# Attention and a maxout feed-forward on one core: the first four chunks' scores by pairs of heads, head 0's transposes first, and a new written order

## The chip, the core and the metric

The kernel runs on one core of a Trainium2 chip. The metric is the device time of one execution in microseconds (us). Three runs of the kernel before took 449.90, 450.04 and 452.39 us, median 450.04. The engines are named as in the profile: PE (TensorE matmuls; PEld its weight loads), DVE (VectorE), ACT (ScalarE), POOL (GpSimd) and SP (SyncE, which issues most DMAs; its queue is SPq).

## The reference

Eight batches, eight heads, 576 positions, 64 values per head, all float32.

```python
scores = scale * np.matmul(q, k.transpose(0, 1, 3, 2))
thresh = np.max(scores, axis=-1, keepdims=True) - tau          # tau = 0.02
scores = np.where(scores >= thresh, scores, -1000000000.0)
scores = scores - np.max(scores, axis=-1, keepdims=True)
attn = np.exp(scores)
attn = attn / (np.sum(attn, axis=-1, keepdims=True) + 1e-09)
attn_out = np.matmul(attn, v)
x = attn_out.transpose(0, 2, 1, 3).reshape(4608, 512)
h = np.maximum(np.maximum(x @ w1, x @ w2), x @ w3)              # 512 -> 768
out = h @ w_out                                                 # 768 -> 512
```

## The kernel before

**Tiles.** The work of attention comes in 16 quads, a quad being four heads of one batch. In a quad, r (0 or 1) is a pair of heads and i (0 or 1) the head in the pair, so the head is 2r + i. The 576 queries of a head are nine blocks of 64. A quad has nine chunks of 128 query rows: chunks 0 to 3 are four double blocks of i = 0, chunk 4 is the ninth block of both i, chunks 5 to 8 are i = 1. Each chunk has two tiles, one for each pair r: 128 queries by 576 keys. That makes 288 tiles.

**Steps of a quad.** `load` fetches q and k (the main eight blocks, and the ninth blocks in a transfer of their own) and v (`vm`, and the rests `vr`). `transposed` turns q or k of one pair on PE into a PSUM bank; `evacuated` copies it to SBUF, q by ACT with the scale (`qt`), k by DVE (`kt`). `swapped` has POOL copy `qt` to `qs` with the two halves of the partitions exchanged. `scores` then makes a tile from `kt` with `qt` and `qs`.

**Softmax of a tile.** A tile goes one of two ways, as the string `MASKED` says. Either way DVE takes the row maximum from PSUM ("m", `maximum`) and ACT makes a first pass ("e", `exponents`). For a tile with a 1 (masked) the second pass is on DVE ("k", a `scalar_tensor_tensor`); for a tile with a 0 it is on ACT ("n", an `activation` with an accumulator). DVE takes the reciprocals of a chunk's two sums ("r"), POOL normalizes both tiles into `P` ("p"), SP sends a DMA transpose of `P` to `ptq` ("t"). A tile's buffer `z` is used again four chunks later (`ZBUFS`), once POOL has read it.

**After attention.** `product` ("O") multiplies `ptq` with v; its copies ("x" on ACT, "w" on DVE) make `xt`. `ffn` has 18 hidden pieces for each part of a batch ("F", second half "B"; PE `ph`), whose copy "h" is ACT's and whose maxima "v" are DVE's, and output pieces (`po`, copies "u" on ACT, stores "o"). "g" loads a weight piece, "z" casts it on POOL, "y" casts v on POOL, "l" issues one load of a later quad. The last batch is split in two parts (`SPLIT`).

**Order.** `ORDER` is a string of these letters. The kernel goes through it and issues each step; S, T, O and F carry the number of the PSUM bank they use (four banks, each of 128 x 1024 float32). The helper `_Ordered` chains the instructions of each engine, so every engine runs its own in the order of the string, and an instruction that waits holds up all behind it on its engine. S takes the next tile, T the next transposes ("a" is then the copy of q, "c" of k, "q" one of the swaps). Every recorded instruction has line 90 in the profile, so groups are told apart by tile names.

**The start.** Ahead of `ORDER`, 14 warming transposes (`WARM`) run on PE, the first quad is loaded (`load(0, first=True)`: q on SP, k on ACT's queue), and all of its transposes are written out: q and k of pair 0, then 5 more warming ones (`FILL`), then q and k of pair 1, each with its copies and swaps. One swap copy of the first quad is DVE's, and one k copy is ACT's. The string starts with a weight load and the second quad's loads; the second quad's first transposes (T0) stand behind four score tiles.

Of the kernel before, what the change touches and what calls it, by code (L numbers as in the profile page):

```python
# [24 lines left out]
101000100110000110011100001010010001100010001000101000010000100000100010  # L25
000011110101100001001001001001000001011100101011000110001010010000010011
001010011101100000101100100001001010000110011111000001000100000110000101
001001001101100000110001000100101000001100010011100101110110000001111111
# [4 lines left out]
FILL = 5  # L33
# [6 lines left out]
glllllS0lylS1mylyeS2zmlkS3lelmnlT0mS1aS2rmeqS0meqmeS3pnkT1pT0nrcaptemS0yeS1mgS2eympeS3mqtnT1S0mqnS2knrceprmS  # L40
1epkepeS3mnyS0rkptemnS2pmnlzmS3erremtpT0empS1eklpaS2kgnS0ptnmeprrmlS1epS3mleS2pmlS0eplmetpmeS1knS3tkernkS2pt
nmnprmtepmS1eqS0melpmT2ntrmT3pnrcpatekS3pekS2eqnrS1mtnqmS0pemepS3tmeqS2kepT1lnrcnprtmS0nT1pmS3epmgS2atpmeO1k
yermeO0knptrerT3wpnT2cS1aptmnS3pS2xmptS1emzS0emeS3zgmeS2lrmpnS0lmO1eplmeplknO3qlnrwleplkS1xqgS2ertmF3npF0meT
1pBrteBkyhS2cpnS3mpS1nvF2npmF0eqBmeqBrrvepS3tkhT2pS1nmS0lapmetS2pmeS3mzeF0mF1ezgBrnF2vpgnBktByeF0rvhpS3ntS2p
mF1npmBeBqrveT3zncT0F2taqvS3nBpmnS0tprhS1rmpeS3mtpS2emeyS0mteF1zmeF3kBelqBnvgF2pngT0vBnqlrS1cphS3lrmnS0plmO2
eplmeptS1ewpS3nmF0znmS2lBezkgO3etymyS1vegkF0ntF2nrrmpBxBpveS3phS0mtnF1prmeBprS2evptS3nmF0pnS1mplBermS3ztnS2v
nzS1meS0tmpeF3mperkS2petBmepmS0tkuF1ukelkT3elBkntrarmpS2uS3pmulS0eymtO1empnrO2kpewS3xpS1elmpF2lmF0eyqBrlkeT3
ytBhcF1pnT2vT3qlaBclnS0qvlS2nqtF3mnyF1meS0pBemBthrrF2kpeS3vnBpmF0nS1pveBrprS3mhtS2pmeS0pmeS1tpmF2emF3peBtkeT
0BvaF1onvqT2T0tBcqaS3nkqS0lhrmS2nlpmF1elpF3meBlkBelF0vntS2rvnBpS1mhplS3melF0mS2teBrmepS1rkpO3emnqO2tnrvpnwyS
0xlprS3emoF2pmoT1eyBpctS3evyF0nS1mtnS2pmBeympF1hkS3eyF2rekT0ptBamBnpS0veF3qtvS1urmnpS2mF3epketT0nkT1Bnrmparr  # L50
cpS2uS1pumtS0empS3emqoS1eF2mqlemqleS3kplnS0mBlepmlekT1teO3kunktO0urcpnrrwlS2nplS1xmpS3lmpS0eompS1eF2mtpeF3me
BkBetS0khF1nrmF2pnBvpBerrvS3phS0mtnpS1mF2peS3mtpeBmeF1yvF0etByknBvnS2tS3rhmpS1melpS0meF3lmF2elBkeBlvT1ntF0nv
T3BacS2ohS1rrmlpnF3lmF0peoBkpeBovnT2oS1qavS3tnprO2rmpmleqS0wtnT3pS1mepO2mteqkeqF0nS1cxBympnS3rS2hytmS1emF0pe
F3mpeBrkBpetF2vnF1pBnvS0thkS3nmF2BmeBveF0rrvpT1uS3kapS0nmS2F1pmtepmeS3rktepS0mnS2pmlBelrmeplS3kupS0lurmS2elp
F1mnoqmeS0qreS2lmpS3elmBpelmptekO0nketO2ukurrnwpT3T1xpcS0aF2ymyT3tpS1ceBqmS3thqF0meF2pknBtBnvF1nS3rtrvpeBmS0
phS2lmepS1lmyS3etF0meyF2mpeBkBetF1knF3vnBBrvhpS0nvT1pF2nmF3takBeS0rvplBmS1phlrS2remplF3mpleF0klBpeS1lvnS2lpm
nBtrO3mepvnptS2nwS1emF0mF3eBrkepS2hBrmS1nptvS0npT2meO3qmeycqlT0xT1yS2lacF3ntmyT0yeF1kqBatrBrevqF0hkS2pnoS3mF
1pmBteBpveS2qntS0vpnF3mprS1mlueS3pmoS0nqmtF2epmekT1oBerocpetrkS3npS1nmS0lpumS3uopmS1eT2mF0aokeorS3remplS2emt
pS1emBpeklqtkO3uqunO0rtmpewpT2xtS3cpeS0mnF2tF1meBknF3lkBhlBevF2nS0vnBmS1hrrS3pmeF0pmS2eBpmteF1pveF3kBlnS0vnl
S2rrBnmlpS1hrlmpF0eF3mtpeBkpBevtS2nF1pvnT0pBtmaS3hS0metF1rmepT2BrcepS3nvptT0S2nmyS1amS3lepmS0leO2mlelmeO1rkp  # L60
ewnT3pF0xcF2nykBnS1vnBrmS3phF0rrmepS2BynmqF1levF3qlBekpF0onvS2tBqmBhqrS1lepvT2S3lampF0lmS2peoBkpetF1vnS3prmu
S0ntqmS1eF2pmetpmeS3rkepS1tBmnpmelrS0keptS3muS1uymS0temT2yeF3pcntknT2BkelramtpS1nS2pmuS0leqrmO1tuqrkepO3nwep
mS1xpS2metF3pmS0eqBmeF1yhrkT2pBtecF3nS0vpnlS2rmpS1nlmBpnF0lveS2tmF3eBmeBkleF1klhF2lnrBvplS0nrrvptBnS3mphS1my
teS2mF3epmF0eBpeBtvpT1nrS2yvnlS3maF0omnqS1kBepF3temS2hpBrrmeS0ptveS1pmS3nptS2meO0pmeymnqlO3weokeoF1xkT0tT2S3
rcapBnmlF2pnS0vqtBerrmpS1hF3mqeT2BpncF0evptF2nkBpT1nvBlaS3ylS0hmoF1yqmT2eoBqrcnF0tpS3ervT2pBmaF1ytkqS2uvnS3q
mS1epF0mepmeS2kteT3BrnrcponmpS1uryS3umtS2emF0pepomeS1opnS2mtpeO3myektnO1wnkS2xrS3repmS1mpBekpteS2muS3purmF1e
pF0tmeBpkS3ntBhS2rnmpO1empO3xvS2xtnkS1eF3rmpF0emByepBveF1tkS2hS3mBmF0eF2rvepBBpvS1htkO3nmO0xkS2xeS3rmF0pF1me
pBeBtvS2F3vF0mF1kBeBkhF2nrvBpnBrvpS3hS0ptmS1pmeS2mtnF0mF3eBrnpBvnF1pS2vntS0rmpBmF3phoS2eS0omeF1tmBeBkO2vO0rv
pF3kpF1uketeF3kekBwrrkpBukxpuF2F0hptF1vF2pvF0hF1tvF2rvpF0hF1vpF2vF0thF1uvF2uvF0hoF3vF1vF2hoF0voO3oO1wovF2xF3
uoF0F1hF2vF0vF1hF2vF0vF1hF2vF0vF1hF2vF0vF1hF2vF0vF1hF2vBvF0uuooBF1uuuooo  # L70
# [31 lines left out]
def kernel(  # L102
# [22 lines left out]
    nc = tc.nc  # L125
# [56 lines left out]
    def load(g, first=False):  # L182
        b, qd = quads[g]
        L = Ls[g] = dict(b=b, qd=qd, first=first)
# [7 lines left out]
        q2 = nc.scalar if first else sync  # L192
        srcs = (("q", q, sync), ("k", k, q2))
        if first:
            for n, src, e in srcs:
                e.dma_start(out=L[n][:, 0:8], in_=rows_of(src)[:, 0, 0:8])
        for n, src, e in srcs:
            e.dma_start(out=L[n][:, 8:10], in_=rows_of(src)[:, :, 8])
            yield
        for n, src, e in srcs:  # L200
            if first:
                e.dma_start(out=L[n][:, 10:18], in_=rows_of(src)[:, 1, 0:8])
            else:
                e.dma_start(out=L[n].rearrange("p (r c) d -> p r c d", r=2)[:, :, 0:8], in_=rows_of(src)[:, :, 0:8])
            yield
# [37 lines left out]
    def swapped(L, r):  # L243

        cols = slice(320 * r, 320 * r + 64 * (5 - r))
        for x in (1, 0) if L["first"] else (0, 1):
            e = vector if L["first"] and (r, x) == (0, 0) else pool
            e.tensor_copy(out=L["qs"][64 * x:64 * x + 64, :, cols],
                             in_=L["qt"][64 - 64 * x:128 - 64 * x, :, cols])
            yield  # L250
# [7 lines left out]
    def transposed(L, n, r):  # L258
# [3 lines left out]
        nj = 5 - r  # L262

        def first(where):
            st["ps"] = ps = bank("tp", where)
            main = ps.rearrange("p (i z) -> p i z", i=2)[:, :, 0:256].rearrange("p i (jj u x) -> p i jj x u", jj=2, x=2)
            for j in range(nj):
                for i in (1, 0):
                    rows = slice(64 * i, 64 * i + 64)
                    tensor.transpose(main[:, i, j // 2, j % 2] if j < 4 else ps[:, 512 * i + 256:512 * i + 320],  # L270
                                     couple(L, n, r, j, rows), identf[rows, rows])
# [435 lines left out]
```

## Time and profile before

| | |
|---|---|
| median of three runs | 450.04 us (449.90 to 452.39) |
| profiled execution, its own time | 449.93 us |
| its span, first to last instruction | 448.1 us |
| DMA | 87.44 MB, mean 195 GB/s |
| q and k loads of 512 KB | 4.7 and 5.1 us from issue to landing (medians) |
| DMA transposes of P | 144, 4.2 us to landing (median) |
| mean granted PE clock | 0.988 |

The span is what the profile sees; the 1.83 us to the execution's own time lie around it. Group rows name an operation by "out<-in". Times in timelines are from the span's start: start, length, engine, operation, and in brackets how long the engine had been idle and what released it.

### The profile page before, as it was taken

To read this page: it belongs to the slowest core of one execution; us is meant where nothing else is said; L and a number is where in the kernel's file an instruction comes from. 1 tells how busy PE (TensorE), PEld (TensorE's weight loads), DVE (VectorE), ACT (ScalarE), POOL (GpSimd) and SP (SyncE) were. 2 spreads that over 40 slices of the span, in tenths; PEclk is the share of its full clock that TensorE was granted. 3 is DMA by queue.
4 is the path that set the end of the run, shared out by engine and by line. 5 is a ranking of instruction groups with operands and counts; after the bars stand their busy time and mean duration, and the time that the engine had idled before them with its cause. 6 is when DMAs were issued, how large, how long until landed. Compare 5 with 4: busy or idle time off the path is not lost.

```text
span 448.1 us, 14065 instructions
## 1 busy us (share of the span) xinstructions
PE 427.0 (95%) x5195; PEld 317.6 (71%) x5195; DVE 399.4 (89%) x1101; ACT 392.4 (88%) x793; POOL 314.2 (70%) x417
## 2 busy tenths in 40 slices
PE   7766889999999999999999999999999999999995
PEld 6524647767688768878687867868687787787762
DVE  3799999899999999999999999999999999999641
ACT  3899999999899999999999999999999999866422
POOL 3798889989785985587776785659777787534400
PEclk9898899999999999999999999999999999999999
DMA  8989999999999999999999997999998999546722
GB/s 235 266 195 188 234 238 190 249 244 220 250 192 193 187 236 209 207 215 179 227 175 205 228 217 176 217 230 205 197 195 203 204 156 194 108 78 132 130 95 107
DMA packets 212773, 87.44 MB, mean 195 GB/s; under 512 B 185824, under 2 KB 199648, under 8 KB 212704
## 3 DMA queue, kind: packets, MB, share of 16 engines
q1 hardware_dynamic: 212000, 85.69, 94.6%
q8 instruction: 41, 0.67, 0.6%
q10 hardware_dynamic: 704, 0.85, 0.6%
q14 instruction: 28, 0.23, 0.2%
HBM read 34.60 MB, written 9.44 MB: 98 GB/s over the span
## 4 chain that ended last, share of the span: by engine, by line
PE 77%; DVE 7%; ACT 5%; POOL 3%; DMA 3%; issue 2%; SPq 1%; DVEq 0%; POOLq 0%; ACTq 0%
PE ph L90 30%; PE sc L90 28%; PE po L90 10%; PE o L90 7%; ACT z L90 5%; DVE z L90 4%; PE tp L90 3%; DVE unused L90 2%; POOL P L90 2%; DMA qm<-in_q_dram 1%; DMA km<-in_k_dram 1%; SPq L90 1%; DVE hm L90 1%; DMA out_dram<-ob 1%; DVE kt L90 0%
## 5 line engine op out<-in xcount | busy, mean ns | idle before, releaser
L90 POOL TENSOR_SCALAR P<-z,rs 128x576 bf16<-128x576 f32 x288 | 228.8, 809 | 89.2 <-DVE rs L90 45.2
L90 PE MATMUL sc<-kt,qs 64*128 64x256 f32 (+2 forms) x640 | 180.5, 423 | 7.7 <-DVE z L90 2.0
L90 PE MATMUL sc<-kt,qt 64*128 64x320 f32 (+2 forms) x640 | 181.1, 433 | 4.0 <-DVE kt L90 1.2
L90 PE MATMUL ph<-xt,w 64*128 64x288 bf16 (+2 forms) x2160 | 165.5, 283 | 0.4 <-DVE hT L90 0.2
L90 PEld LDWEIGHTS <-w 64*128 64x128 bf16 (+1 forms) x2160 | 127.3, 94 | 29.8 <-issue 7.2
L90 ACT ACTIVATE z<-sc,nm 128x576 f32<-128x576 f32 x179 | 128.9, 740 | 10.8 <-DVE unused L90 9.5
L90 DVE TENSOR_SCALAR_CACHE_REDUCE unused<-sc 128x576 bf16<-128x576 f32 x179 | 130.5, 751 | 8.2 <-PE sc L90 7.3
L90 ACT ACTIVATE z<-z 128x576 f32<-128x576 f32 x179 | 120.8, 680 | 0.1
L90 PEld LDWEIGHTS sc<-kt,qs 64*128 64x128 f32 (+1 forms) x640 | 92.3, 179 | 30.9 <-ACT z L90 7.8
L90 PEld LDWEIGHTS sc<-kt,qt 64*128 64x128 f32 (+1 forms) x640 | 92.2, 178 | 20.0 <-ACT z L90 5.4
L90 DVE SCALAR_TENSOR_TENSOR z<-z 128x576 f32<-128x576 f32 x109 | 89.1, 832 | 0.2
L90 DVE TENSOR_SCALAR_CACHE_REDUCE z<-sc 128x576 f32<-128x576 f32 x109 | 80.5, 752 | 7.9 <-PE sc L90 4.6
L90 ACT ACTIVATE z<-z,nm 128x576 f32<-128x576 f32 x109 | 81.5, 772 | 2.6 <-DVE z L90 2.0
L90 POOL COPY qs<-qt 64x512 f32<-64x512 f32 (+1 forms) x63 | 45.0, 714 | 15.0 <-ACT qt L90 11.9
L90 PE MATMUL po<-wo,hT 64*128 64x512 bf16 (+1 forms) x480 | 54.0, 356 | 0.1
L90 DVE TENSOR_TENSOR hm<-ph,hm 128x576 bf16<-128x576 f32 (+2 forms) x54 | 37.1, 687 | 11.7 <-PE ph L90 11.3
L90 ACT ACTIVATE hm<-ph 128x576 bf16<-128x576 f32 (+2 forms) x54 | 32.1, 595 | 15.2 <-PE ph L90 13.7
L90 PEld LDWEIGHTS <-hT 64*128 64x128 bf16 (+1 forms) x480 | 29.3, 97 | 17.0 <-issue 3.1
L90 DVE TENSOR_TENSOR hT<-ph,hm 128x576 bf16<-128x576 f32 (+2 forms) x54 | 37.2, 688 | 3.8 <-PE ph L90 0.9
L90 PE MATMUL o<-ptq,vb 128*64 128x512 bf16 (+2 forms) x544 | 38.9, 282 | 0.2
L90 ACT ACTIVATION_READ_ACCUMULATOR z<-z 128x1 f32 x179 | 35.4, 198 | 0.0
L90 PEld LDWEIGHTS <-vb 128*64 128x64 bf16 x544 | 23.5, 111 | 14.4 <-issue 4.4
(33 smaller groups left out, 278.2 us busy)
## 6 DMA issues: line engine op xcount, KB each, us to landing
vm<-in_v_dram SPq DMA_DIRECT2D x32, 256.0 KB, 4.2
out_dram<-ob SPq DMA_DIRECT2D x31, 256.0 KB, 2.8
qm<-in_q_dram SPq DMA_DIRECT2D x15, 512.0 KB, 4.7
km<-in_k_dram SPq DMA_DIRECT2D x15, 512.0 KB, 5.1
stage<-in_moe_w_dram SPq DMA_DIRECT2D x9, 512.0 KB, 4.5
ptq<-P SPq DMA_TRANSPOSE x144, 4.2
stage<-in_moe_w_out_dram SPq DMA_DIRECT2D x3, 512.0 KB, 4.9
qm<-in_q_dram SPq DMA_DIRECT2D x16, 64.0 KB, 2.9
```

The lines of the kernel that those rows point to most:

```text
L90: ins = fn(*a, **kw)
```

## The change

- The order of tiles: the first four chunks have all their r = 0 tiles first (tiles 0 to 3), then their r = 1 tiles; from chunk 4 on the two tiles of a chunk follow each other as before.
- Ahead of the string only head 0 (r = 0, i = 0) of the first quad is transposed: q without its ninth block (4 transposes) and k (5). Then come 6 warming transposes (`FILL`, before 5), and the two swaps of these columns. The rest of the first quad comes by T in the string: head 2, then heads 1 and 3, six steps of 4 or 5 transposes. So the first quad has eight smaller copies out of PSUM where it had four.
- All k copies are DVE's and all swaps POOL's, also in the first quad.
- The first loads of the first quad: each queue sends pair 0's main blocks first; then SP sends q's pair 1 ahead of q's ninth blocks, and ACT's queue k's ninth blocks ahead of k's pair 1.
- `MASKED` (107 ones in place of 109) and `ORDER` are new throughout.

```diff
-FILL = 5
+FILL = 6
...
-glllllS0lylS1mylyeS2zmlkS3lelmnlT0mS1aS2rmeqS0meqmeS3pnkT1pT0nrcaptemS0yeS1mgS2eympeS3mqtnT1S0mqnS2knrceprmS
+glS2llS3mlyS0lemlT1emlT2akT3elqcT1qlaT0qlcS2aqgT3nzS1lcnT0mS3qgamqeS0qmeS1ymT2ynqkT0eS3ncarmT2peS0mpermpetS1
...
+            for x in range(3):
+                for n, src, e in (("q", q, sync), ("k", k, nc.scalar)):
+                    if x == 0:
+                        e.dma_start(out=L[n][:, 0:8], in_=rows_of(src)[:, 0, 0:8])
+                    elif (x == 1) == (n == "k"):
+                        e.dma_start(out=L[n][:, 8:10], in_=rows_of(src)[:, :, 8])
+                    else:
+                        e.dma_start(out=L[n][:, 10:18], in_=rows_of(src)[:, 1, 0:8])
...
-        elif L["first"] and r == 1:
-            scalar.activation(out=dst(L["kt"]), in_=src, func=AF.Copy)
...
+    def blocks(n, r, ii):
+
+        if n == "q" and ii == (0,):
+            return ((0, 1, 2, 3), (4, 0, 1, 2, 3))[r], 256 * r
+        return ((0, 1, 2, 3, 4), (0, 1, 2, 3))[r], 320 * r
+
+    def swapped(L, r, ii=(0, 1)):
+
+        js, off = blocks("q", r, ii)
+        cols = slice(off, off + 64 * len(js))
+        for x in (0, 1) if len(ii) == 2 else (1, 0):
+            pool.tensor_copy(out=L["qs"][64 * x:64 * x + 64, ii[0]:ii[-1] + 1, cols],
+                             in_=L["qt"][64 - 64 * x:128 - 64 * x, ii[0]:ii[-1] + 1, cols])
             yield
...
+    tiles = [(n, r) for r in range(2) for n in range(4)] + [(n, r) for n in range(4, len(steps)) for r in range(2)]
+    place = {x: n for n, x in enumerate(tiles)}
...
-    for x, (r, n) in enumerate(((0, "q"), (0, "k"), (1, "q"), (1, "k"))):
-        p = transposed(Ls[0], n, r)
+    for x, n in enumerate("qk"):
+        p = transposed(Ls[0], n, 0, (0,))
         p.first(x)
         p.done[0]()
...
+    for _ in range(FILL):
+        tensor.transpose(warm[:, 0:128], identf, identf)
+    for _ in swapped(Ls[0], 0, (0,)):
+        pass
...
-                T=((g, n, r) for g in range(1, NQ) for r in range(2) for n in "qk"),
+                T=iter([(0, n, 1, (0,)) for n in "qk"] + [(g, n, r, (0, 1) if g else (1,)) for g in range(NQ) for r in range(2) for n in "qk"]),
```

More of the change, by code (lines that the diff above doesn't have):

```diff
@@ L45 @@
[L45 to L54, printed above, removed]
@@ L256, in targets, with transposed @@
                 L["qs"] = qk.tile([128, 2, S], F32, name="qs")
-    def transposed(L, n, r):
+    def transposed(L, n, r, ii=(0, 1)):
         st = {}
-        nj = 5 - r
+        js, off = blocks(n, r, ii)
+        lead = 64 if js[0] == 4 else 0
         def first(where):
             st["ps"] = ps = bank("tp", where)
-            main = ps.rearrange("p (i z) -> p i z", i=2)[:, :, 0:256].rearrange("p i (jj u x) -> p i jj x u", jj=2, x=2)
-            for j in range(nj):
-                for i in (1, 0):
+            main = ps.rearrange("p (i z) -> p i z", i=2)[:, :, lead:lead + 256] \
+                .rearrange("p i (jj u x) -> p i jj x u", jj=2, x=2)
+            for j in js:
+                for i in ii[::-1]:
                     rows = slice(64 * i, 64 * i + 64)
-                    tensor.transpose(main[:, i, j // 2, j % 2] if j < 4 else ps[:, 512 * i + 256:512 * i + 320],
+                    ninth = 512 * i + (0 if lead else 256)
+                    tensor.transpose(main[:, i, j // 2, j % 2] if j < 4 else ps[:, ninth:ninth + 64],
                                      couple(L, n, r, j, rows), identf[rows, rows])
@@ L553, with pieces_of_scores @@
         pass
[L554 to L555 removed]
+    for x, n in enumerate("qk"):
+        p = transposed(Ls[0], n, 0, (0,))
         p.first(x)
         p.done[0]()
[L558 to L570 removed]
+    for _ in range(FILL):
+        tensor.transpose(warm[:, 0:128], identf, identf)
+    for _ in swapped(Ls[0], 0, (0,)):
+        pass
+    def pieces_of_scores():
+        for n, r in tiles:
+            if n == len(made):
+                g, idx = steps[n]
+                made.append(dict(g=g, idx=idx, n=n))
+            yield made[n], r
     def pieces():
```

117 lines of the change are left out of this document (52 added, 65 removed).

## The prediction, as it was put on record

> **What bounds the kernel now.** I read the page first, then the table of windows, the timeline of the first 22 us, the chain of waits and the order of both kernels' instructions on each engine. The page:
>
> ```profile
> span 448.1 us, 14065 instructions
> ...
> PE 427.0 (95%) x5195; PEld 317.6 (71%) x5195; DVE 399.4 (89%) x1101; ACT 392.4 (88%) x793; POOL 314.2 (70%) x417
> ...
> PE   7766889999999999999999999999999999999995
> ...
> PEclk9898899999999999999999999999999999999999
> ```
>
> PE is busy 427.0 of 448.1 us. Its 21 idle us lie at the two ends. Windows place them:
>
> ```profile
> 20.00:57.00 37.00, 27.69 (x237) 17.11 (x232) 35.96 (x109) 36.60 (x77) 32.79 (x42) 0.91 1.00 202
> 57.00:70.00 13.00, 11.63 (x135) 7.13 (x136) 12.46 (x36) 12.62 (x27) 11.55 (x15) 1.00 1.04 232
> 70.00:100.00 30.00, 29.64 (x372) 21.25 (x366) 28.40 (x74) 29.24 (x63) 27.93 (x36) 1.00 1.15 226
> 100.00:443.70 343.70, 343.18 (x4334) 260.47 (x4332) 311.76 (x855) 302.46 (x611) 232.04 (x309) 1.00 0.94 187
> ```
>
> Columns: stretch, length, busy PE, PEld, DVE, ACT, POOL, granted clock, DMA share, GB/s. From 100 to 443.7 us PE idles 0.52 us: no order can gain more there. From 20 to 57 us PE idles 9.31 us, ACT only 0.40 and DVE 1.04: the softmax of the first 50 score tiles bounds, because the feed-forward matmuls (first at 67.9 us) are not yet to be had. Whatever brings ACT and DVE through these tiles sooner brings the end nearer, one for one. The last 4.4 us are the output.
>
> Before that comes the start:
>
> ```profile
> 9.40 0.78 ACT L90 ACTIVATE z<-z,nm 128x576 f32<-128x576 f32 x1 [0.55 <-DVE z L90]
> 10.74 0.74 ACT L90 ACTIVATE z<-sc,nm 128x576 f32<-128x576 f32 x1 [0.56 <-DVE unused L90]
> 11.51 0.68 ACT L90 ACTIVATE z<-z 128x576 f32<-128x576 f32 x1
> 12.10 0.19 ACT L90 ACTIVATION_READ_ACCUMULATOR z<-z 128x1 f32 x1
> 13.99 0.70 ACT L90 ACTIVATE qt<-tp 128x640 f32<-128x640 f32 x1 [1.70 <-PE tp L90]
> ```
>
> ```profile
> 11.00:13.40 2.40, 0.00 (x0) 0.00 (x1) 1.94 (x7) 1.26 (x3) 1.98 (x3) 1.00 0.94 333
> 13.40:17.00 3.60, 3.57 (x26) 3.30 (x28) 1.79 (x5) 3.01 (x5) 2.03 (x3) 0.61 1.11 332
> ```
>
> By 13.99 us ACT has done two first passes (e, 0.78 and 0.74) and one second pass (n, 0.68; its accumulator read overlaps, so instructions in a row are 0.67 to 0.69 apart). Then it, DVE and PE stand behind the second quad's first transposes, whose q lands at 13.29:
>
> ```profile
> 0.74 4.12 DMA km<-in_k_dram
> ...
> 7.90 5.39 DMA qm<-in_q_dram
> 13.29 0.14 issue
> 13.43 0.53 PE tp L90 x10
> ```
>
> **The change, part by part.**
>
> *First scores.* Before, 10 q and 10 k transposes run from 4.64 (0.064 apart), 5 warming ones from 5.95 to 7.21 (0.25 each), then 16 more transposes, and the first score matmul at 7.81, its maximum on DVE at 8.60. After: 4 q and 5 k transposes, 6 warming ones, scores. The k transfer lands at 4.86, so transposes end at about 4.9 + 5 x 0.064 = 5.2 (5.95 if the ninth block's transfer comes as late as the old transposes could hide). Copies: DVE kt took 0.82 at 640 columns and 0.67 at 512, so 0.45 at 320; ACT qt 0.70 and 0.60, so 0.39 at 256; POOL qs 0.71 and 0.61, so 0.41. kt and the first qs half are ready near 6.1, hidden under the warming ones, which end at 5.2 + 6 x 0.25 = 6.7. Scores start at 6.7 (bounds 6.1 and 7.5), the first maximum at 7.5: 1.1 us sooner.
>
> *ACT up to 13.99.* The transfer that ends at 13.29 doesn't move: SP issues the same kinds of transfer in the same places up to it (three q, two v, two v rests, weights, two rests, q). Only q's two last pieces of the first quad swap; they are wanted at about 8 us, and the old first quad's were in use by 7.2. The new ACT order ahead of that wait is e, e, three q copies of the remaining heads, an e among them, and two n. From 8.2: 5 x 0.68 + (0.44 + 0.44 + 0.39) = 4.7, done at 12.9, before 13.99. So three e and two n are done where there were two and one: ACT leads by 2 x 0.68 = 1.36 us (bounds: 0 if k is 1.4 late, 1.36). The kt copy taken off ACT (0.59) and the split q copies (1.66 for 1.30) fall into idle time: 0.
>
> *DVE.* Four kt copies (0.45, 0.37, 0.45, 0.37) replace one of 0.82 and a qs copy of 0.52: +0.3, in time in which DVE idled (1.16, 0.57 and 1.88 us). Five maxima are done by the wait, not four: lead 0.68.
>
> *POOL.* Eight qs copies, 4 x 0.41 + 4 x 0.46 = 3.5 us, for 0.71 + 1.28 = 2.0: +1.5. POOL idled 1.7 us just before the second quad's copy at 14.82, and the first normalization (16.40) stood behind that copy before as after. 0; without that gap up to 1.5.
>
> *Masks.* 107 of 288 tiles are masked, not 109. It is the early part that counts: 15 and 14 in the first two groups of 48 tiles, before 17 and 16. Each tile unmasked puts an n on ACT (0.68 in a row) and takes a second pass of about 0.75 from DVE. At tile 48 ACT has 1.36 more and DVE 1.5 less to do; at tile 96 twice that.
>
> *Net at the first feed-forward matmul.* ACT: 1.36 - 1.36 = 0. DVE: 0.68 + 1.5 = 2.2 sooner. The two wait for each other (in the chain ACT z carries most of 34 to 45 us, DVE z of 49 to 60), so the bounds are 0 and 2.2 and I take the middle: -1.1. From 57 to 100 us ACT gets 1.36 more and has 0.38 + 0.76 = 1.14 idle: +0.2.
>
> *The rest of the order.* It is rewritten throughout, but tile counts hardly move: first product at tile 40 in both, first feed-forward piece at 50, the 30th at 98, the 100th at 215. From 100 us on, bounds -0.5 and, for new waits, the largest of the rows of this stage, about +2; I take 0. At the end two products and two pieces go ahead of the last scores, so the last softmax has about 17.4 - 1.4 - 1.7 = 14.3 us of PE work to hide under. It needs three maxima and four second passes (4.9), some 1.6 of maxout, two normalizations (1.5) and a DMA transpose (4.2): 12.2. Covered by 2.1; 0.
>
> Sum -0.9. The profiled execution took 449.93 us (span 448.1 and 1.8 around it), 0.11 under the median of 450.04. 449.93 - 0.9 = 449.0.
>
> *A rule against it.* PE idles 2.57 us before 13.43 and is granted only 0.61 of its clock until 17, and score matmuls of 0.38 and 0.43 take 0.63 and 0.74; pairs come 0.53 apart instead of 0.27. The new order has many short waits from 8 to 13 us in place of one long one, so the clock could fall sooner. The Trainium skill (TensorE: Matmul & The Clock Gate, What's actually happening) has the clock halve after an idle window of about 3.4 us; the trace agrees in kind, but here a wait of 2.57 us was enough. By that rule the clock would hold, since no wait so long is left, and the sum stay at 449.0; by the row it can still fall, at the price of the clock rival below.
>
> **Rivals.**
>
> *All of the lead arrives.* If DVE was the true limit up to 57 us and ACT's idle time takes in its extra passes, the gain is the 2.2 plus the part of the start that is not in it (1.1 - 0.68): 2.6, 447.3 us. For: DVE ends most waits from 49 to 60. Against: ACT's 36.60 of 37.
>
> *ACT becomes the limit (slower).* Place: tiles 1 to 96. If nothing of DVE's relief counts, ACT ends them 4 x 0.68 - 1.36 = 1.36 later: 451.3. It decides from the point where ACT's idle time up to 100 us (1.5 us now) is used up. For: ACT at 99% from 20 to 57 us. Against: idle 0.76 at 70 to 100.
>
> *A late k load.* The third quad's main k transfer stood ahead of the first DMA transpose on SP (issued at 14.84); now it stands behind three, each of which waits for POOL's P, so it goes at about 25 us and lands at 30 to 31 (5.1 to 6.1 by its own rows). Its transposes come after tile 22, near 31 to 32; behind them PE's scores and so DVE and ACT queue. From a landing at 33 on each us costs one. 452 with 2 us.
>
> *The clock.* Eight tiles at 0.53 a pair for 0.27, two pairs each, 4.2 us if PE bounds then: up to 453.2. Against: DVE needs about 1.4 a tile, so PE has room for slow scores.
>
> *The change does not do what it says:* if the ninth block of k lands so late that scores still start near 7.8, only masks and order are left, and ACT's 1.36 is not repaid: 451.3, as above.
>
> **How the numbers follow.** Forecast 449.0 (its own range 448.0 to 450.4): 0.47. Whole lead, 447.3: 0.22. ACT as the limit, or no earlier scores, 451.3: 0.14. Late load, 452: 0.08. Clock, 453.2: 0.04. Something in the new order that I don't see, of either sign: 0.05. 446.0 to 452.5 holds all but some 0.15. A measurement of this kernel tells about 1%, 4.5 us, from no change: faster than 445.5 takes more than any case gives, 0.05; slower than 454.5 the clock's worst or an unseen stall, 0.06; within, 0.89.
>
> **What would show it.** First score matmul at 6.7 and first maximum at 7.5; three e and two n on ACT ahead of the second quad's q copy, still at about 14; ACT over 99% busy from 20 to 57; first feed-forward matmul 0 to 2 us sooner than 67.9; PE idle after 100 us still near 0.5; no PE wait for km near 31. I am wrong if the first feed-forward matmul moves by more than 3 us, if PE idles over 2 us from 100 us to its last matmul, or if the final product waits for a DMA transpose.

## The result, and the profile after

The kernel after takes 454.49 us (median of 12 runs, 451.18 to 455.98). Twelve runs of the kernel before on the same chip have a median of 450.69 us. The ratio is 1.0073, with a 95% interval of 1.0047 to 1.0099: slower by 3.3 us going by the ratio (0.0073 x 450.7) and 3.8 by the medians, where 1 us less was forecast. The profiled execution took 453.53 us (before 449.93), so the two profiles differ by 3.6 us and can be held side by side.

The page of the after:

```profile
span 451.7 us, 14092 instructions
...
PE 429.6 (95%) x5196; PEld 311.1 (69%) x5196; DVE 400.7 (89%) x1099; ACT 394.3 (87%) x798; POOL 314.2 (70%) x422
...
PE   8776889999999999999999999999999999999995
...
PEclk9987999999999999999999999999999999999998
```

The first slice is fuller than before (8 for 7), as it was meant to be, and so is the third (7 for 6); the second and the fourth are as they were. What has changed on the path that sets the end is in the shares of the chain, first the before's, then the after's:

```profile
PE ph L90 30%; PE sc L90 28%; PE po L90 10%; PE o L90 7%; ACT z L90 5%; DVE z L90 4%; PE tp L90 3%; DVE unused L90 2%; POOL P L90 2%; DMA qm<-in_q_dram 1%; DMA km<-in_k_dram 1%; SPq L90 1%; DVE hm L90 1%; DMA out_dram<-ob 1%; DVE kt L90 0%
```

```profile
PE ph L90 29%; PE sc L90 28%; PE po L90 10%; ACT z L90 8%; PE o L90 8%; PE tp L90 3%; DVE z L90 2%; DVE unused L90 1%; DMA qm<-in_q_dram 1%; DMA km<-in_k_dram 1%; POOL P L90 1%; SPq L90 1%; DVE hm L90 1%; DMA out_dram<-ob 1%; DVE kt L90 0%
```

ACT's passes over z hold 8% of the chain instead of 5%, DVE's z, its unused and POOL's P half of what they held. The stretches that were shown of before (busy PE, PEld, DVE, ACT, POOL, granted clock, DMA share, GB/s):

```profile
20.00:57.00 37.00, 27.89 (x218) 16.63 (x218) 34.93 (x103) 35.62 (x75) 34.67 (x43) 0.86 1.01 208
57.00:70.00 13.00, 10.83 (x122) 6.32 (x119) 11.98 (x28) 11.89 (x26) 10.68 (x14) 1.00 0.80 190
70.00:100.00 30.00, 29.20 (x375) 21.79 (x373) 27.61 (x74) 29.85 (x65) 27.15 (x37) 1.00 1.06 232
100.00:447.20 347.20, 345.93 (x4355) 254.59 (x4351) 313.90 (x861) 304.29 (x613) 231.86 (x309) 1.00 0.92 184
```

From 20 to 57 us ACT and DVE are each busy 1 us less than before (35.62 for 36.60, 34.93 for 35.96): they wait more. POOL has become full too (34.67 for 32.79). After 70 us PE idles 0.80 + 1.27 = 2.07 us, before 0.36 + 0.52 = 0.88.

The difference at PE's end (447.28 for 443.71 us, +3.57) adds up so: the first feed-forward copy on ACT starts at 72.06 for 69.96, +2.10; PE idles 1.19 more after 70 us; 0.28 is left for everything else.

**The start** did what was forecast in this execution (in half of those profiled it did not, see the last section). ACT's timeline:

```profile
8.39 0.78 ACT L90 ACTIVATE z<-z,nm 128x576 f32<-128x576 f32 x1 [2.58 <-DVE z L90]
9.07 0.73 ACT L90 ACTIVATE z<-sc,nm 128x576 f32<-128x576 f32 x1
...
10.02 0.74 ACT L90 ACTIVATE z<-sc,nm 128x576 f32<-128x576 f32 x1
...
11.60 0.68 ACT L90 ACTIVATE z<-z 128x576 f32<-128x576 f32 x1
...
12.27 0.67 ACT L90 ACTIVATE z<-z 128x576 f32<-128x576 f32 x1
...
13.87 0.70 ACT L90 ACTIVATE qt<-tp 128x640 f32<-128x640 f32 x1 [0.84 <-PE tp L90]
```

Three e and two n ahead of the second quad's q copy, which waits for a transfer that hasn't moved (chain of the after):

```profile
0.74 4.10 DMA km<-in_k_dram
7.87 5.30 DMA qm<-in_q_dram
```

Windows of the same stretch: PE is busy 3.82 us of 5.20 where it did nothing for 2.4, and its clock here stays whole until 17 us (0.61 before).

```profile
8.00:13.20 5.20, 3.82 (x40) 2.72 (x36) 4.36 (x14) 4.42 (x10) 3.73 (x6) 1.00 1.00 313
13.20:17.00 3.80, 3.19 (x40) 2.43 (x40) 2.89 (x7) 3.13 (x6) 2.98 (x7) 1.00 1.02 299
```

**Where the lead goes.** Starts of the same instruction, after less before, in the profiled executions (us):

| | DVE m | ACT e | POOL P |
|---|---|---|---|
| 1st | -1.01 | -1.01 | +2.00 |
| 16th | -2.73 | -1.15 | -0.62 |
| 24th | -1.25 | +0.88 | -1.93 |
| 36th | +0.12 | +1.69 | -1.27 |
| 44th (m), 50th (e) | +1.48 | +2.10 | |

DVE is 2.7 us ahead at its 16th maximum, and ACT 1.15 ahead at its 16th first pass (28.2 us). By 37.8 us ACT is behind. Two places can be seen. In the first, PE, ACT and the clock (PE's timeline of the after, then ACT's, then a window):

```profile
29.02 0.55 PE L90 MATMUL sc<-kt,qs 64*128 64x320 f32 x1 [2.09 <-ACT z L90]
...
31.74 0.75 PE L90 MATMUL tp<-identf,qm 64*128 64x64 f32 x9
```

```profile
32.64 0.70 ACT L90 ACTIVATE qt<-tp 128x640 f32<-128x640 f32 x1 [0.73 <-PE tp L90]
```

```profile
29.40:32.80 3.40, 3.40 (x31) 2.48 (x28) 3.15 (x10) 2.43 (x7) 3.20 (x5) 0.50 0.98 234
```

PE waits 2.09 us for a bank that ACT's first pass gives back, is granted half its clock from 29.4 to 32.8, and its third-quad transposes come late for ACT, which stands 0.73 us. The second place is DVE's, beside POOL (DVE's timeline, then POOL's):

```profile
57.57 3.15 DVE L90 SCALAR_TENSOR_TENSOR z<-z 128x576 f32<-128x576 f32 x1
60.65 0.75 DVE L90 TENSOR_SCALAR_CACHE_REDUCE unused<-sc 128x576 bf16<-128x576 f32 x1
```

```profile
55.35 2.80 POOL L90 TENSOR_SCALAR P<-z,rs 128x576 bf16<-128x576 f32 x3
58.09 1.03 POOL L90 CAST w<-stage 128x1024 bf16<-128x1024 f32 x1
59.08 1.04 POOL L90 CAST vb<-vm 128x1024 bf16<-128x1024 f32 x1
```

One second pass k takes 3.15 us for some 0.75. It starts inside POOL's last P, and ends 0.6 us behind the second of two casts that follow that P without a gap. The k before it started at 55.31, just ahead of POOL's P at 55.35, and took 0.77; there POOL's three P's take 2.80 where they need 0.75 each. The Trainium skill (SBUF — State Buffer, SBUF: two separate sides) says that DVE, with two inputs in SBUF, and a POOL instruction that reads SBUF share one port pair: whichever starts first locks it for its whole instruction, and the other waits outright. The trace agrees where two start together: the k that started first kept its length (0.77) and POOL's P's beside it took 2.80 for 2.25; the k that started inside a P took 3.15. That this pass lost the pair to the two casts as well, which started after it, is an inference from where it ends.

**What ACT's time to its 50th first pass consists of** (sums over the trace, us):

| | e | n | qt, kt copies | idle | 50th e at |
|---|---|---|---|---|---|
| before | 32.69 | 19.34 (29) | 5.25 | 9.69 | 69.33 |
| after | 32.54 | 21.35 (32) | 4.88 | 10.30 | 71.42 |

(The table load and two xt copies, 2.36 us, are the same in both.) Three more n are 2.01 us. Idle time is up by 0.61 although the start took off 1.01, so 1.6 of waits are new. ACT's timeline shows where they are: from 20 us on it idles 2.47 us (before 0.77). Of these 0.73 is the gap at 32.64 above, 0.33 and 0.24 are waits for DVE at 47.34 and 29.84, and 1.11 comes behind the long second pass of DVE:

```profile
61.50 1.42 ACT L90 ACTIVATE z<-sc,nm 128x576 f32<-128x576 f32 x2 [1.11 <-DVE unused L90]
```

DVE, to its 50th maximum: 14 k for 17, yet 15.56 us for 14.64 (1.11 each for 0.86), and k copies 5.75 for 4.17. The relief that was forecast for DVE is not there at all.

### The profile page after: what moved, and what is told of

It reads as the page before. It is cut to its first block, busy times and chain, and to the rows that moved or that the text cites. A ratio compares the mean times of both kernels' runs of the same rounds, so it can differ in the third digit from the quotient of the medians.

```text
span 451.7 us, 14092 instructions
## 1 busy us (share of the span) xinstructions
PE 429.6 (95%) x5196; PEld 311.1 (69%) x5196; DVE 400.7 (89%) x1099; ACT 394.3 (87%) x798; POOL 314.2 (70%) x422
## 4 chain that ended last, share of the span: by engine, by line
PE 78%; ACT 9%; DVE 5%; issue 3%; DMA 3%; POOL 1%; SPq 1%; DVEq 0%; POOLq 0%; ACTq 0%
PE ph L90 29%; PE sc L90 28%; PE po L90 10%; ACT z L90 8%; PE o L90 8%; PE tp L90 3%; DVE z L90 2%; DVE unused L90 1%; DMA qm<-in_q_dram 1%; DMA km<-in_k_dram 1%; POOL P L90 1%; SPq L90 1%; DVE hm L90 1%; DMA out_dram<-ob 1%; DVE kt L90 0%
## 5 line engine op out<-in xcount | busy, mean ns | idle before, releaser
L90 PE MATMUL sc<-kt,qs 64*128 64x320 f32 (+2 forms) x640 | 182.1, 423 | 6.3 <-ACT z L90 5.0
L90 PE MATMUL sc<-kt,qt 64*128 64x256 f32 (+2 forms) x640 | 182.0, 433 | 5.5 <-ACT z L90 4.4
L90 PEld LDWEIGHTS <-w 64*128 64x128 bf16 (+1 forms) x2160 | 126.0, 94 | 32.1 <-issue 6.8
L90 ACT ACTIVATE z<-z 128x576 f32<-128x576 f32 x181 | 122.1, 680 | 0.2
L90 DVE SCALAR_TENSOR_TENSOR z<-z 128x576 f32<-128x576 f32 x107 | 91.0, 864 | 0.0
L90 ACT ACTIVATE z<-z,nm 128x576 f32<-128x576 f32 x107 | 79.8, 773 | 9.4 <-DVE z L90 9.1
L90 DVE TENSOR_SCALAR_CACHE_REDUCE z<-sc 128x576 f32<-128x576 f32 x107 | 78.9, 752 | 10.0 <-PE sc L90 7.2
L90 POOL COPY qs<-qt 64x640 f32<-64x640 f32 (+3 forms) x68 | 46.9, 690 | 11.6 <-ACT qt L90 8.2
L90 PE MATMUL po<-wo,hT 64*128 64x512 bf16 (+1 forms) x480 | 52.9, 356 | 0.1
L90 ACT ACTIVATE hm<-ph 128x576 bf16<-128x576 f32 (+2 forms) x54 | 32.0, 593 | 17.2 <-PE ph L90 16.7
L90 PEld LDWEIGHTS <-hT 64*128 64x128 bf16 (+1 forms) x480 | 26.3, 97 | 20.1 <-issue 3.7
```

The lines of the kernel that those rows point to most:

```text
L90: ins = fn(*a, **kw)
```

## Experiments

All are compared with the before, run beside them; the after stands at 1.0073 [1.0047, 1.0099]. Tiles are counted from 0.

### Parts of the change, alone

Four tiles (9, 20, 31, 44) of the before unmasked, so that four second passes go from DVE to ACT, in their old places:

```diff
-101000100110000110011100001010010001100010001000101000010000100000100010
+101000100010000110010100001010000001100010000000101000010000100000100010
```

> The kernel before with four tiles of the first 48 (tiles 9, 20, 31 and 44) taken from the masked way to the other one, each at its old place in the order: four second passes move from DVE to ACT. Theory A (ACT alone sets the pace of the first 100 us, so each second pass on it costs its 0.68 us): 2.7 us slower than before, and the 50th first pass on ACT 2 to 2.7 us later than the 69.3 us of before. Rival B (the loss lies in stalls of the new order, not in the masks): within 0.7 us of before.

Measured: 453.69 us, ratio 1.0064 [1.0041, 1.0087]. To the 50th e ACT's n take 21.97 us (before 19.34), and that e starts at 71.81, +2.5. DVE's k fall to 13 and 10.0 us; DVE idles instead (17.2 us for 11.1). More n on ACT reach the end in full, and DVE's relief is worth nothing: theory A's number.

The opposite in the before, tiles 12, 23, 33 and 43 masked:

> The opposite of the four-more experiment: in the kernel before, tiles 12, 23, 33 and 43 get the masked way, each second pass at its old place, so four of them move from ACT to DVE. Theory A (ACT alone sets the pace of the first 100 us): up to 2.7 us faster than before, 448 us. Rival D (the written order is balanced so finely that any departure from it, either way, costs about 3 us, and the count on ACT has no part in it): slower than before by 1 to 3 us.

Measured: 451.85 us, ratio 1.0039 [1.0014, 1.0065]. ACT's n fall to 16.81 us, but its idle time rises from 9.69 to 14.00. Theory A alone is false: ACT now waits for DVE instead (5.3 us for its z, unused and rs from 8 to 75 us, before 1.7). Rival D's number (1 to 3 us slower) is met too; the next run decides on it. Two each way (20 and 31 unmasked, 23 and 33 masked):

> The kernel before with two second passes moved from DVE to ACT (tiles 20 and 31) and two from ACT to DVE (tiles 23 and 33), so each engine's count is as it was. Theory A: within 0.7 us of before. Rival D: 1.5 us slower or more.

Measured: 451.10 us, ratio 1.0010 [0.9992, 1.0028]. So it isn't that any departure from a written order costs 3 us, and rival D is false; the balance between the two engines counts.

The new start (first 15 tiles of the after's order) with the before's order and masks behind it, and the reverse:

```diff
-...S2pnmS1perpmtnS3qmeS2pmleS1S0rmeplknplnrkleptem...
+...S2pnmS1perpmtnlyyqeS3yS0rnpemnS2pmklzmS3erremtpT0emp...
```

> The changed kernel's start (head 0 first, its first 15 tiles with their order and masks), then the order and masks of before. Theory A and rival B both: the start's lead of about 1 us is kept, 449 to 450 us against 450.7 of before. Rival C (the start itself loses what it wins, by more and smaller copies and a later first normalization): 451 us or more.

Measured: 453.94 us, ratio 1.0079 [1.0049, 1.0108]: rival C's number. In the profiled execution (452.31 us, the fastest of six) the first maximum is 1.31 us sooner than the before's, the 16th still 0.34, the 20th 1.73 later, and so it stays. The place, on DVE:

```profile
27.95 0.76 DVE L90 TENSOR_SCALAR_CACHE_REDUCE z<-sc 128x576 f32<-128x576 f32 x1 [2.29 <-POOL P L90]
```

A maximum that writes a z waits for POOL to have normalized the chunk four before. POOL's first P starts at 18.41, as in the after, for 16.40 before: with all r = 0 tiles first, chunk 0 has both sums only after its r = 1 tile, the fifth of the order. Three casts of v (24.8 to 27.2 us) stood ahead of that P as well.

> The start of before (all of the first quad's transposes ahead, its first 15 tiles with their order and masks), then the changed kernel's order and masks. Theory A and rival B both: the loss without the lead, 455 to 456 us. Rival C: the loss was in the start, so 451 us.

Measured: 454.96 us, ratio 1.0086 [1.0061, 1.0110]. ACT has the after's 21.28 us of n, and the 50th e starts at 72.85 (after 71.42, which had the start of 1.2 us sooner). So the new order loses as much with the old start, 3.9 us by the ratio. Whether the new start gives some of that back (3.3 us for the after) the intervals don't tell. With the casts of new_start_old_rest moved behind (three y to ahead of tile 24, a z to ahead of tile 26):

> The new start with the old rest, 453.9 us, but POOL's casts of the second quad's v, and the weight cast behind them, stand some eight tiles later, behind the normalizations that were waiting for them. Theory E (the new start finishes a chunk only with its fifth tile, so POOL's first normalization comes 2 us later, and with the old place of the casts the z buffers come free 2.3 us late, which DVE waited for at 28 us): that wait goes, and with it 2 to 3 us, 451 us or less. Rival C (the start loses its lead in some other way): still 453 to 454 us.

Measured: 453.01 us, ratio 1.0057 [1.0034, 1.0080]: rival C's number, not theory E's 451. On the spot DVE's wait is 0.73 us instead of 2.29, but the time is lost elsewhere: the 24th maximum is 0.64 us behind the before's, the 30th 2.18. (In this execution the first maximum was at 8.90, not 7.29; see the last section.) The 0.9 us between the two medians lies within the intervals, so that the casts cost time at the end is not shown.

The after's order with the before's masks from tile 8 on:

> The changed kernel with the old masks from tile 8 on, every second pass at its place in the new order, only on the other engine where the mask differs. Theory A: the four extra second passes in the first 96 tiles are gone, 2.7 us, so 451 to 452 us where the changed kernel takes 454.5. Rival B (the new order's own stalls: the scores held up at 27 us, half clock from 29 to 33, a 3.15 us pass on DVE at 57.6): still 454 us or more.

Measured: 484.46 us, ratio 1.0748. That is far beyond both theories, although B's "454 us or more" covers it. PE idles 11.5 us from 100 to 250 us, where it idles 0.95 in the after: the loss is spread over the whole program, presumably since n and k stand in places that were made for other masks. The run tells nothing of A against B.

### Taking ACT's passes back, in the after

Tiles 10, 16, 29 and 40 of the after masked:

```diff
-100010100000011000011100000110001001100000101000001100000000010000000110
+100010100010011010011100000111001001100010101000001100000000010000000110
```

> The changed kernel with tiles 10, 16, 29 and 40 on the masked way, each second pass at its place: its early count on ACT comes down to that of before. Theory A: the changed kernel's 454.5 us less 2 to 2.7 us, 452 us. Rival D: 455 us or more.

Measured: 457.29 us, ratio 1.0166 [1.0136, 1.0195]. ACT's n fall to 18.58 us, below the before's, but ACT idles 15.08 us (9.5 of them waiting for DVE from 8 to 75 us, in the after 4.2) and its 50th e starts at 74.13: theory A, as a remedy, is false. DVE has 18 k (16.97 us) and 10 k copies in the same stretch.

### Repairing the two places

POOL's copy of v at 59.08 later by some ten of its instructions:

```diff
-...S3nmygxrlrme...S0pgx...
+...S3nmgxrlrme...S0pygx...
```

> The order of the kernel after with one instruction elsewhere: the bf16 copy of V that POOL makes at 59.08 us, straight behind a weight copy, is made some ten instructions of POOL later. Nothing is left out. Theory F (the loss of about 1 us between 57 and 61 us is VectorE's: its second pass of 3.15 us at 57.57 lasts until POOL's copies at 58.09 and 59.08 are through): that pass takes 2 us or less, VectorE's 50th first pass starts 1 us or more sooner than the after's, and the time is 0.7 to 1.5 us under the after's, about 453.3 where the after is 454.5. Theory G (ScalarE alone is the limit there, with 0.3 us of waits between 57 and 70 us): the pass is shorter, VectorE waits by as much more, and the time is that of the after within 0.4 us.

Measured: 454.23 us, ratio 1.0075 [1.0050, 1.0100]. On the spot theory F holds. The same k on DVE, and POOL beside it:

```profile
59.44 0.98 DVE L90 SCALAR_TENSOR_TENSOR z<-z 128x576 f32<-128x576 f32 x1
60.35 0.75 DVE L90 TENSOR_SCALAR_CACHE_REDUCE unused<-sc 128x576 bf16<-128x576 f32 x1
```

```profile
58.35 1.46 POOL L90 TENSOR_SCALAR P<-z,rs 128x576 bf16<-128x576 f32 x2 [0.97 <-ACT z L90]
59.76 1.55 POOL L90 CAST w<-stage 128x1024 bf16<-128x1024 f32 x1
```

0.98 us for 3.15, and now the POOL cast that starts inside it is the long one (1.55 for 1.03). Between its 40th and 44th maximum DVE gains 2.2 us on the after. At the end nothing is left of it: 1.0075 for 1.0073, theory G's number. The first maximum of this execution is 1.34 us later than the after's, but only 0.40 of that is left at its 20th first pass, so it can't hide much. The gain went into DVE's waits, as G has it: idle to its 50th maximum 13.62 us for 11.26.

The two n at 26.90 and 27.56 (and the reciprocals and the normalization that need them) behind the next two e, so that PE gets its bank sooner:

```diff
-S0rmeplknplnrkleptem
+S0rmeplkplkletenrpnm
```

> The order of the kernel after with ScalarE's two sums of exponentials at 26.90 and 27.56 us moved behind the next two first passes (28.23 and 28.85), so that these give their banks back 1.4 us sooner. Nothing is left out. Theory H (TensorE's wait of 2.09 us for a bank at 26.9 is what brings the half clock at 29.4 to 32.8, and that the late transposes and ScalarE's idle 0.73 us at 32.64): the wait falls under 1 us, the clock stays whole until 35, the gap ahead of ScalarE's copy of the fourth quad's q falls under 0.3, ScalarE's 24th first pass starts 0.5 to 0.9 sooner, and the time is 0.5 to 0.9 under the after's if nothing later takes it. Theory E (POOL's normalization, late by 2 us since the first chunk is done late, sets the buffers that VectorE's first passes wait for): the normalization that needs the second of the moved sums is a further 1 us late, VectorE waits for a buffer at about 31 us for 1 us more, and the time is that of the after or up to 1 us over it.

Measured: 455.53 us, ratio 1.0105 [1.0077, 1.0132]. PE's wait there fell from 2.09 to 1.0 us, and still its clock was at half from about 31 to 44 us, with the same gap of 0.74 us ahead of ACT's q copy (the third quad's, not the fourth's as the expectation says). By itself the move does not keep the clock up. Both moves together:

> Both of the moves above in one kernel: the V copy of POOL later and the two sums of ScalarE behind two first passes. Nothing is left out. If both theories F and H hold, the gains add up: 1.2 to 2.4 us under the after's, 452.1 to 453.3 where the after is 454.5, which still leaves 1.5 us or more over the before. If ScalarE's added second passes alone (2.0 us by the 50th first pass) are the loss, the time is that of the after within 0.5 us.

Measured: 454.44 us, ratio 1.0076 [1.0046, 1.0107]. In this execution, with a wait of 0.9 us, the clock stayed whole:

```profile
29.40:32.80 3.40, 1.79 (x19) 0.78 (x18) 2.79 (x9) 3.07 (x9) 3.07 (x5) 1.00 1.14 313
```

ACT is busy 3.07 us here instead of 2.43, and its gap ahead of the q copy is gone. Up to this point the order is that of after_e_before_n and only the clock differs, so the half clock did make that gap. But that it stayed whole looks like luck. PE has the same two waits in both (1.02 and 1.59 us there, 0.91 and 1.59 here). In the clock records of the traces the clock keeps one value for stretches that are all multiples of 3.413 us long (but for the last of each trace). Such a step begins at another time in each execution: there one step, from 27.54 to 30.96 us, holds most of both waits (PE busy 42% of it), here a step ends between them, at 28.90, and PE is busy 53% of the next. From 20 us to its 50th e ACT now idles 0.76 us, as in the before (0.77). The gain goes on: ACT's 50th e is 1.38 us sooner than the after's, its 82nd still 0.86 sooner, and the 86th is level. Between them lies one wait of PE (name, total, times, longest):

```profile
PE tp L90 <- DMA qm<-in_q_dram: 0.8, 1, 0.8
```

The sixth quad's main load of q stands on SP behind three DMA transposes of P (issued at 109.79, in the after at 110.60). In the after PE comes to it only just too late to wait. A new limit stood behind the old one. The time is the after's within 0.5 us, which the expectation had for the case that only ACT's passes count; the trace shows that a lead was there and was lost. The load ahead of those transposes, in the after, then with the moves:

```diff
-...S1elrprO3mtepmeF0pkxtS2epS3mnBtF1pnvBznmS0lev...
+...S1ellrprO3mtepmeF0pkxtS2epS3mnBtF1pnvBznmS0ev...
```

> The order of the kernel after with one DMA elsewhere in SP's queue: the main load of q for the sixth quad, at 110.60 us behind three transposes of P, is issued ahead of them, about 6 us sooner. Nothing is left out. In the profiled execution of the after its transposes start at 115.56, no sooner than the load's landing allows, but TensorE's idle time from 100 to 250 us is 0.95 in all. Theory J (this load is a second limit at 115 us, for which whatever the first 100 us give is lost): TensorE's idle time from 110 to 120 us falls to nothing, and the time is 0 to 0.4 us under the after's, since the after comes to this point only just too soon. Theory K (the load is no limit): no difference over 0.3 us and the same idle time.

Measured: 453.94 us, ratio 1.0087 [1.0063, 1.0111]: no gain alone, as both theories allowed.

> The V copy of POOL later (as in after_vcast_later) and the load of q sooner (as in after_load_sooner), in one kernel. Nothing is left out. Theory J with F: the 2.2 us that the V copy's move gives VectorE between its 40th and 44th first passes now come through to the end as far as ScalarE lets them, and the time is 0.7 to 1.5 us under the after's. Theory K: the time of after_vcast_later, which was 0.3 us under the after's, within 0.3.

Measured: 453.68 us, ratio 1.0079 [1.0059, 1.0099]. By the medians that is 0.8 us under the after, by the ratios 0.3 over it: no gain that can be told from none, so neither theory is decided.

> All three moves: V copy later, the two sums of ScalarE behind two first passes, load of q sooner. Nothing is left out. In after_both_moves the profiled execution was 1.4 us ahead of the after's at ScalarE's 50th to 82nd first passes (0.7 against 2.1 over the before's at the 50th), and level with it from the 86th on, where TensorE waited 0.8 us for this load. Theory J: the lead stays, ScalarE's 100th first pass is 0.7 to 1.2 over the before's instead of 2.1, and the time is about 1.3 us under the after's, 452.6 to 453.4 where the after is 454.4. Theory K: the lead is lost at another place before the 100th first pass, and the time is that of after_both_moves within 0.3.

Measured: 453.78 us, ratio 1.0084 [1.0063, 1.0106]. Its profiled execution is 0.68 us ahead of the after's at the 50th e and still 0.74 ahead at PE's last matmul. In this execution the lead comes through, as theory J has it, but it is half of what was expected: the 100th first pass is 1.52 us over the before's, not 0.7 to 1.2, and the clock fell again (half from 31.80 to 35.22 us). In the time nothing is to be seen of it: the ratio is not under the after's.

The same V copy in the before (54.12 us, beside a k of 1.68 us), behind the next normalizations:

> The order of the kernel before with the V copy that POOL makes at 54.12 us made after the next five normalizations. Nothing is left out. In the before, VectorE's second pass at 54.09 us, beside this copy, takes 1.68 us. If a copy of POOL makes the pass beside it long, the pass now takes 1.0 us or less, and the time is 0.4 to 0.9 us under the before's, about 449.8; if ScalarE alone sets the pace there, the time is the before's within 0.3. This is the version that could be under both kernels.

Measured: 449.90 us, ratio 0.9992 [0.9970, 1.0014]. That k now takes 0.76 us, and the time is the same within 0.3%. No version tried is faster than the before beyond what the interval allows.

### Giving DVE passes where it waits

Tiles 17 and 24 masked, whose n DVE waits for, in the after; then in after_vcast_and_load, where DVE has room; then four (17, 24, 40, 47):

```diff
-100010100000011000011100000110001001100000101000001100000000010000000110
+100010100000011001011100100110001001100000101000001100000000010000000110
```

> The kernel after with two more tiles masked (the 18th and the 25th), so that VectorE makes the second passes for which it waits 0.99 us at 33.05 and 0.3 us at 40.5. Nothing is left out. Theory A (ScalarE's added second passes, 2.0 us by its 50th first pass, are the loss): ScalarE has 1.35 us less by then and the time is about 1.3 us under the after's. Theory L (both engines are full, and what one gives up the other has no room for): VectorE takes 1.5 us more, the 3.15 us pass beside POOL's copies stays, and the time is that of the after or up to 1.5 us over it.

Measured: 455.69 us, ratio 1.0115 [1.0089, 1.0141]. ACT's n fall by 1.25 us, its idle time to the 50th e rises by 2.5. ACT and DVE stand for POOL and for each other (ACT's timeline, then DVE's):

```profile
37.78 0.74 ACT L90 ACTIVATE z<-sc,nm 128x576 f32<-128x576 f32 x1 [0.76 <-POOL P L90]
39.30 0.78 ACT L90 ACTIVATE z<-z,nm 128x576 f32<-128x576 f32 x1 [0.78 <-DVE z L90]
```

```profile
38.50 0.76 DVE L90 TENSOR_SCALAR_CACHE_REDUCE z<-sc 128x576 f32<-128x576 f32 x1 [1.20 <-POOL P L90]
```

A masked tile's maximum writes z, so it needs POOL's P first; an unmasked one's does not.

> The same two tiles masked in the kernel with POOL's V copy later and the load of q sooner (after_vcast_and_load), where VectorE has about 2 us of room before its 44th first pass. Nothing is left out. Theory A with F: now VectorE has the room, ScalarE's 50th first pass starts 0.9 to 1.3 us sooner than in after_vcast_and_load, and the time is 0.7 to 1.3 us under that one's, about 2.3 to 2.9 over the before's. Theory L: no gain over 0.3 us.

Measured: 454.20 us, ratio 1.0083 [1.0058, 1.0107]: no gain.

> As the last, with four tiles masked (the 18th, 25th, 41st and 48th), which makes the number of ScalarE's second passes by its 50th first pass about that of the before. Nothing is left out. Theory A with F: 1.5 to 2.5 us under after_vcast_and_load, 1.2 to 2.0 over the before's, whose start and copies it does not have. Theory L: VectorE becomes the limit, and the time is over that of after_vcl_2_masked by 0.5 us or more.

Measured: 455.23 us, ratio 1.0104 [1.0080, 1.0127]. Theory L, three times: what ACT gives up DVE can't take, with or without the room.

## Why the prediction was wrong

- *First scores.* Right in the profiled execution: scores at 6.74, first maximum at 7.58 (forecast 6.7 and 7.5). As the kernel's usual time it was too much: see the last section.
- *ACT up to 13.99.* Right: three e and two n, copy at 13.87, ACT's gap ahead of it 0.84 for 1.70.
- *DVE.* Mis-sized. Four smaller k copies and no swap were to cost 0.3 and cost 0.5 (0.49, 0.42, 0.49 and 0.42 for 0.82 and 0.52). By the 50th maximum k copies are 1.58 up and the swap 0.52 down, +1.1: the other 0.6 is a copy of a later quad, at 69.89 us, which the before makes at 70.31, behind its 50th maximum.
- *POOL.* Wrong. "The first normalization stood behind that copy before as after" overlooked what it waits for: both sums of chunk 0. It starts 2.0 us later (18.40 for 16.40), and new_start_old_rest showed what a late P can cost (2.29 us of DVE at 27.95). In the after itself it cost little: from the fifth to the 30th P POOL is 0.6 to 2.7 us ahead of the before, and from 20 to 57 us DVE waits 0.4 us for P (before 0.9).
- *Masks.* Right for tile 48 (15 masked tiles for 17, two more n). By the 50th e, which is where the sum was compared, it is three more n, 2.01 us and not 1.36.
- *Net at the first feed-forward matmul.* This is the step that failed: the choice of -1.1 as the middle between ACT (0) and DVE (2.2 sooner). Measured is +2.10 at ACT's 50th e and +2.09 at DVE's 50th maximum, outside both bounds. ACT's 0 was a lead of 1.36 against two n of 1.36. There were three n (0.65 more), and the lead, 1.15 at the 16th e, was gone by the 24th: ACT's idle time is 0.61 up where the lead would have it 1.36 down (1.97 more). Copies and e are 0.52 less, and 0.65 + 1.97 - 0.52 is the 2.10. The sum had no term for new waits; the rows show two large ones, 0.73 us behind the half clock and 1.11 behind the second pass of 3.15. DVE's 2.2 was counted as if its k kept their length. They went from 0.86 to 1.11 us each, so that three k fewer took 0.9 us more; of the 3.5 us that the longer k make, 2.4 are that one pass beside POOL. before_4_more_on_act shows that even a real relief of DVE (k of 10.0 us) brings nothing when ACT is loaded: the two are no alternatives of which one may take the middle; the later one of each stretch counts.
- *The rest of the order.* "I take 0", with +2 as the bound: PE idles 1.19 us more after 70 us. Its waits there are small ones (0.3 us at 70.63, 77.57 and 140.39, 0.2 at 247.38 and 334.69) which return in the kernels with this order and are not in the before. Between the first feed-forward copy and PE's end lie 374.9 to 376.9 us in the kernels with this later order (after_old_masks aside), whenever that copy starts, and 373.75 in the before.
- *Rivals.* "ACT becomes the limit", 451.3, had the right sign and the right engine, with too small a price: it counted passes and no waits. The late k load did not come: that load was issued at 25.50, as forecast, its transposes ran at 32.3 and waited for nothing of it. The clock fell at another place in the profiled execution (29.4 to 32.8), after a wait of 2.09 us; at the place that the rival named it fell in five other executions with the new start, at 11.1 to 11.8 us for 3.4 or 6.8 us. The Trainium skill (TensorE: Matmul & The Clock Gate, What's actually happening) has it fall after about 3.4 us of idle time; here waits of 2.57 (before) and 2.09 us, and in after_e_before_n one of 1.0, were followed by it. By these traces it is not a single wait that goes with it, but the share of a step of 3.413 us in which PE is busy. In the first 100 us of the twenty traces the clock fell after each of the 24 whole-clock steps in which PE was busy 47% or less, after 14 of the 32 with 48 to 60%, and after 5 of the 410 with more; those five are the ones at 11.1 to 11.8 us.
- *Signs.* ACT was to be over 99% busy from 20 to 57 us and was at 96% (35.62 of 37.00): this sign pointed at the waits. The signs of being wrong were set too wide: the first feed-forward matmul moved by 1.8 us (67.92 to 69.68) and not 3, and PE idled 1.27 us from 100 us on and not 2, in a kernel that is over 3 us slower.

What is shown: more n on ACT reach the end in full (1.0064 with four); fewer are no remedy in either kernel, since ACT then waits for DVE, whose maxima need POOL's P (1.0039, 1.0166, 1.0115); each half of the change's order loses as much as the whole (1.0079, 1.0086); and the two local stalls of the after can be taken away without the time following. By the rows of the profiled execution the loss up to the 50th e is three n and the waits behind the half clock and the long k. What stays open: why the time does not follow when these waits are gone. No repair of one of them gained enough to be measured.

## What to carry to other kernels

Where two engines at 95% and more wait for each other, don't average their terms and don't credit one's relief: add up the busier one's work and its new waits, and ask for each tile moved what the other engine needs for it (here a buffer that a third engine frees). A lead at the start is worth only as much as the next shared resource lets through, so list what each following stage waits for, buffers included, before the lead is carried to the end. This change of the written order could not be halved (1.0079 and 1.0086): masks, places and start belong together, and a stall that is removed may be found to have stood in front of another (here a load, 50 us later).

## What was not expected of the hardware

**The start comes in two forms.** In 14 profiled executions of kernels with the new start the first maximum is at 7.17 to 7.58 us in seven and at 8.73 to 9.25 in the other seven; in six with the old start it is at 8.60 to 9.26. So the forecast gain of 1 us is there in half of them; on the mean it is about 0.65 (8.16 for 8.81). In the later form PE's instructions are slow from about 6 to 10 us, here in after_load_sooner, then in the after:

```profile
6.30 1.54 PE L90 MATMUL warm<-identf 128*128 128x128 f32 x6
...
8.36 0.63 PE L90 MATMUL sc<-kt,qs 64*128 64x256 f32 x1
...
9.25 0.76 DVE L90 TENSOR_SCALAR_CACHE_REDUCE z<-sc 128x576 f32<-128x576 f32 x1 [2.35 <-PE sc L90]
```

```profile
5.93 0.87 PE L90 MATMUL warm<-identf 128*128 128x128 f32 x6
...
7.06 0.38 PE L90 MATMUL sc<-kt,qs 64*128 64x256 f32 x1
```

0.63 for 0.38 is what the same matmul takes at half clock (13.4 to 17 us of the before), though the profile's clock column shows 1.00 from 6 to 10 us. The landing of the loads does not part the two forms (first q transposes at 4.54 to 4.83 in the one, 4.63 to 4.89 in the other). The traces' clock records do: the first whole clock is on record from 4.25 to 5.54 us in the seven early ones and from 9.37 to 10.82 in the seven late ones. The column shows 1.00 ahead of that only because nothing is on record there. With the old start the clock is whole from 4.42 to 7.44 us, in all six ahead of the first score matmul (7.81 or later). So in half of the profiled executions the new start brought the scores ahead of the full clock; why no step between 6 and 7.4 us brought it in these, as it did in three executions with the old start, is open. The shift need not reach the end: after_load_sooner's first maximum is 1.67 us later than the after's, and its last matmuls 1.35; in after_vcast_later 0.40 of 1.34 was left at the 20th first pass.

**A second pass of DVE that started while POOL was at work could take up to 3.15 us** for 0.75. It took 1.68 us in the before (at 54.09), 2.15 in after_vcast_and_load (58.22), 2.73 in before_4_more_on_act (71.95) and 3.15 in the after (57.57), and each of the four ended 0.6 us behind the last of the POOL instructions that followed each other beside it. Moving one of them away brought 3.15 to 0.98. It is not so beside every such series: of the 702 passes in all traces that met two POOL instructions, the middle one took 0.90 us.
